# A fused attention-and-MLP kernel: batch 0's q chain reordered with its fifth tile behind the MLP, batch 1 begun on half its tokens, attention placed between halves of second-layer tiles

## The chip, the cores and the metric

The kernel runs on one core of one Trainium2 chip. The metric is the device time of one execution in microseconds (us). Every number quoted as a kernel's time is a median of several executions. Profiled spans are a little shorter than the timed executions of the same kernel (311.2 us of span against 313.3 us of time), and are compared with spans only.

Engines are named as in the profile: PE is TensorE (matmul), PEld its weight load, DVE is VectorE, ACT is ScalarE, POOL is GpSimd, SP is SyncE, whose queue ("SPq") issues most transfers.

## The reference

Linear attention with cosine weights, followed by an MLP with the activation `h * cos(h)`. There are 8 batches, 8 heads, 576 tokens and 64 channels per head.

```python
def _attn_ref(q, k, v):                      # (8, 8, 576, 64) each
    theta = np.pi / 2.0 * pos / S
    def phi(x, c, s):
        r = np.maximum(x, 0.0)
        return np.concatenate([r * c, r * s], axis=-1)      # the "features", 128 wide
    q_p, k_p = phi(q, cos_w, sin_w), phi(k, cos_w, sin_w)
    kv  = np.einsum('bhsf,bhsd->bhfd', k_p, v)
    z   = np.sum(k_p, axis=2)
    num = np.einsum('bhsf,bhfd->bhsd', q_p, kv)
    den = np.einsum('bhsf,bhf->bhs', q_p, z)[..., None] + 1e-06
    return num / den

x = attn_out.transpose(0, 2, 1, 3).reshape(4608, 512)
h = x @ w_in                                  # 512 x 2048, the first layer
g = h * np.cos(h)
out = g @ w_out                               # 2048 x 512, the second layer
```

## The kernel before

A batch of 576 tokens is worked on as four tiles of 128 tokens and a fifth tile of 64. Two batches share the fifth tile: batch `b` uses the even or the odd partitions of tile slot `NT` (`NT` is 4), by `b % 2`. The raw q, k and v of a batch lie in one landing buffer each, which every batch reuses. Here is how it is loaded and read:

```python
raw = {nm: cpool.tile([P, H, NT + 1, D], F32, name=f"{nm}m") for nm in srcs}  # qm, km, vm

def load(b, name, after=None):
    if b >= B:
        return
    m, n = raw[name], b % 2
    if after is not None:          # a tiny copy on POOL that makes the load wait for `after`
        nc.gpsimd.tensor_copy(out=m[0:2, 0, 0, 0:1], in_=after)
    five, four = tokens(srcs[name][b])
    nc.sync.dma_start(out=blocks(m, n), in_=five)                      # 64 partitions, 5 slots
    nc.sync.dma_start(out=blocks(m, 1 - n)[:, :, 0:NT, :], in_=four)   # the others, 4 slots

def feat(b, name, t, g, act):      # relu(x) * cos or sin; reads all 128 partitions of slot t
    dst = (kps if name == "k" else qps)[b][:, t, :, g, :]
    src, sc = raw[name][:, :, t, :], CS[:, b % 2, g, t:t + 1]
    # ... on ScalarE if act, else on VectorE
```

The table `CS` holds zeros for the partitions of slot `NT` that do not belong to the batch, so what they contain makes no difference to the result.

The chain from features to the first layer's input: `q_trans` transposes a q tile on PE and ScalarE evicts it; `num` multiplies it with `kvz` (a `kv_group` evicted by ScalarE), and VectorE divides; `x_trans` transposes x on PE and ScalarE evicts it into `xT`. From batch 2 on (`b >= NPE`, which is 2), both transpositions are done by transfers instead (`q_trans_dma`, `dma_start_transpose`).

```python
def gate(dst, M1):                 # h * cos(h): cosine on ScalarE, product on VectorE
    n = M1.shape[-1]
    ch = apool.tile([P, SM], F32, name="ch", tag="ch", bufs=4)
    nc.scalar.activation(out=ch[:, 0:n], in_=M1, func=AF.Sin, bias=PIH, scale=1.0)
    flush()
    late.append(lambda: nc.vector.tensor_tensor(out=dst, in0=M1, in1=ch[:, 0:n], op=ALU.mult))
```

`moe1` computes one first-layer tile (128 of the 2048 columns for 512 tokens) and calls `gate`; `moe2_main` one second-layer tile.

Batch 0's front:

```python
for hb in range(2):
    kv_group(0, hb)
for t in T1:                       # T1 is the five tiles, T the first four
    feat(0, "q", t, 0, False)
    feat(0, "q", t, 1, t % 2 == 0)
    if t == 1:
        q_trans(0, 0)
q_trans(0, 1)
# ... num and flush in turn with q_trans(0, 2), q_trans(0, 3), x_trans(0, 0)
x_trans(0, 1)
q_trans(0, NT)
weights_in = w_out_sb[0:2, (G - 3) * NJT // G, 0:1]
for name in ("k", "q", "v"):
    load(1, name, weights_in)      # batch 1, once most weights have arrived
for j in range(2):
    moe1(0, j, 0, SM // 2)         # half tiles on the first 256 tokens
x_trans(0, 2)
# ... more half tiles, x_trans(0, 3), then whole tiles
```

The MLP of batch `s` is interleaved with the attention of batch `s + 1` by a list of side work with start times, in us of PE work:

```python
for s in range(1, B + 1):          # b = s + 1
    # main: first-layer tiles of s, with second-layer tiles of s - 1 between them
    side += [(5.5, lambda: q_trans_dma(b)), (5.6, lambda: load(b + 1, "q")),
             (6.4, lambda: load(b + 1, "v")), (11.6, lambda: load(b + 1, "k")),
             (14.0, lambda: kv_group(b, 0)), (14.8, lambda: kv_group(b, 1))]
    side += [(15.7 + 1.2 * t, lambda t=t: num(b, t)) for t in range(NT + b % 2)]
```

PE, DVE, ACT and SP keep the written order. Semaphore waits are put in automatically, by which operations touch the same part of a buffer.

## Time and profile before

| before | |
|---|---|
| time, median of the first 3 runs | 313.34 us (312.91 to 314.59) |
| span of the profiled run | 311.2 us |
| PE busy | 285.3 us, 92% |
| first MLP tile of batch 0 / 1 / 2 / 3 | 23.9 / 60.6 / 92.3 / 125.4 us |
| PE's largest waits after the start | 3.2 us (batch 2's MLP), 1.4 us (batch 1's) |

First the page: busy time of each engine, with its share of the span and its number of instructions, then PE's row and the clock row of the 40 slices (tenths; 7.8 us per slice).

```profile
span 311.2 us, 5548 instructions
PE 285.3 (92%) x2124; PEld 153.9 (49%) x2124; DVE 185.1 (59%) x457; ACT 179.2 (58%) x301; POOL 27.6 (9%) x55
PE   0389999799959999999999999999999999999994
PEclk9999999999998999999999999999999999999999
```

PE is the bottleneck. After the front, its row dips only at slices 8 and 12; the clock dips once, right after the second. (The clock row reads 9 from the start only because the trace records changes of the clock, and nothing before the first. In before, the first is the rise to full at 23.74 us.) The list of PE's waits says what those dips wait for. Columns: waiting instruction, what released it, then total us, count, and the longest.

```profile
PE KV_0_125 L121 <- DVE V_0_71 L114: 11.1, 1, 11.1
PE M_1262 L207 <- DMA xT_819<-x_3_1232: 3.2, 1, 3.2
PE M_823 L207 <- ACT xT_515 L184: 1.4, 1, 1.4
```

The first is the wait for the first k and v. The second is batch 2's MLP waiting for its transposed x. To see why x is late, follow the transfer queue: the timeline of SP before batch 2's start (start us, duration of the issue, queue, line, what).

```profile
69.90 6.19 SPq L129 DMA_TRANSPOSE qT_818<-qp_816  x1
...
79.60 1.79 SPq L96 DMA_DIRECT2D km<-in_k_dram  x1
...
82.89 1.64 SPq L169 DMA_TRANSPOSE xT_819<-x_0_1153  x1
```

The view of transfers gives 7.8 us from issue to landing for that first x tile, which is issued behind the k load, and 2.4 us for the same transposition in the last batch, when the queue is empty:

```profile
xT_819<-x_0_1153 SPq DMA_TRANSPOSE x1, 7.8
...
xT_2954<-x_0_3177 SPq DMA_TRANSPOSE x1, 2.4
```

The Trainium skill ("DMA: Bandwidth & Descriptors", section "Queues, rings and completion order") says that on each engine that moves data, descriptors are consumed in ring order. The two landings above agree with it.

### The profile page before, as it was taken

What the parts mean: (1) busy time and instruction counts of PE and PEld (TensorE: products, weight loads), DVE (VectorE), ACT (ScalarE), POOL (GpSimd) and SP (SyncE); (2) the same over time, 40 slices, a digit from 0 to 9 for tenths busy, and PEclk for the clock granted to TensorE, in tenths of its full rate; (3) what the DMA queues carried; (4) which work ended last, traced back from release to release, by engine and by line L of the source; (5) the groups of instructions that cost most, each with busy time, mean ns of one, the idle gap of its engine ahead of it and who ended that gap; (6) DMA issues with size and microseconds to landing.
All of it is one profiled execution on the core that took longest, in us unless ns stands there. A gap on an engine that the chain in (4) does not pass through costs nothing.

```text
span 311.2 us, 5548 instructions
## 1 busy us (share of the span) xinstructions
PE 285.3 (92%) x2124; PEld 153.9 (49%) x2124; DVE 185.1 (59%) x457; ACT 179.2 (58%) x301; POOL 27.6 (9%) x55
## 2 busy tenths in 40 slices
PE   0389999799959999999999999999999999999994
PEld 0377447445724454445744554446644554447441
DVE  2677790699737665766937565966757581565000
ACT  2679787399407852875557732884458543566111
POOL 0810001100010101010011101010001101010110
PEclk9999999999998999999999999999999999999999
DMA  7999989409990999279934999099937541010121
GB/s 227 305 208 206 326 275 351 155 2 171 334 256 0 140 332 253 90 145 309 275 101 83 239 368 192 1 206 316 211 97 139 135 86 68 1 67 2 67 103 67
DMA packets 78587, 53.76 MB, mean 173 GB/s; under 512 B 47456, under 2 KB 76128, under 8 KB 78560
## 3 DMA queue, kind: packets, MB, share of 16 engines
q1 hardware_dynamic: 71264, 40.51, 54.8%
q0 software_dynamic: 6848, 12.59, 15.5%
q8 instruction: 17, 0.28, 0.4%
q10 hardware_dynamic: 448, 0.31, 0.3%
q14 instruction: 10, 0.08, 0.1%
HBM read 36.74 MB, written 9.44 MB: 148 GB/s over the span
## 4 chain that ended last, share of the span: by engine, by line
PE 79%; ACT 7%; DVE 6%; DMA 5%; issue 2%; SPq 0%; ACTq 0%; DVEq 0%
DMA vm<-in_v_dram 2%; DMA xT_1258<-x_3_1575 1%; ACT ch L197 1%; ACT qT_108 L139 1%; PE M_3707 L233 1%; PE M_3064 L233 1%; PE M_2210 L233 1%; PE M_1726 L233 1%; PE M_2584 L233 1%; PE M_699 L233 1%; PE M_3645 L233 1%; PE M_3489 L233 1%; PE M_2931 L233 1%; PE M_2486 L233 1%; PE M_2140 L233 1%
## 5 line engine op out<-in xcount | busy, mean ns | idle before, releaser
L207 PEld LDWEIGHTS <-w_in_sb 128*128 128x128 f16 x536 | 51.2, 98 | 60.8 <-issue 8.2
L265 POOL DMA_DIRECT2D out_dram<-ost x14 | 7.4, 530 | 211.8 <-ACT ost L259 211.8
L219 PEld LDWEIGHTS <-w_in_sb 128*128 128x128 f16 x256 | 14.7, 98 | 0.9
L121 PE MATMUL KV_0_125<-V_0_71,kp_105 128*128 128x65 f16 x20 | 1.6, 240 | 11.6 <-DVE V_0_71 L114 11.1
L257 DVE COPY ost<-M_3707 128x256 f32<-128x256 f32 x1 | 0.4, 424 | 19.7 <-ACT ost L255 19.7
L112 ACT ACTIVATE V_0_71<-vm 128x512 f16<-128x512 f32 x17 | 10.7, 635 | 0.1
L233 PEld LDWEIGHTS <-g_3357 128*128 128x128 f16 x64 | 6.3, 98 | 7.5
L233 PEld LDWEIGHTS <-g_2957 128*128 128x128 f16 x64 | 6.2, 98 | 7.3
L233 PEld LDWEIGHTS <-g_1654 128*128 128x128 f16 x64 | 6.2, 98 | 7.3
L233 PEld LDWEIGHTS <-g_2512 128*128 128x128 f16 x64 | 6.2, 98 | 7.3
L233 PEld LDWEIGHTS <-g_1261 128*128 128x128 f16 x64 | 6.2, 98 | 7.1
L233 PEld LDWEIGHTS <-g_2099 128*128 128x128 f16 x64 | 6.2, 98 | 7.1
L233 PEld LDWEIGHTS <-g_322 128*128 128x128 f16 x64 | 6.1, 98 | 6.8
L233 PEld LDWEIGHTS <-g_822 128*128 128x128 f16 x64 | 6.0, 98 | 6.9
L112 ACT ACTIVATE V_1_72<-vm 128x512 f16<-128x512 f32 x15 | 9.2, 627 | 0.0
L121 PEld LDWEIGHTS <-kp_105 128*128 128x128 f16 x40 | 2.3, 130 | 11.7 <-ACT kp_105 L104 11.1
L266 POOL DMA_DIRECT2D out_dram<-ost x14 | 7.6, 543 | 0.3 <-issue 0.3
L274 POOL DMA_DIRECT2D out_dram<-ostr x8 | 4.3, 545 | 37.0 <-ACT ostr L271 37.0
L104 ACT ACTIVATE kp_105<-km,CS 128x512 f16<-128x512 f32 x5 | 3.2, 709 | 4.6 <-DMA km<-in_k_dram 4.6
L106 DVE TENSOR_SCALAR kp_105<-km,CS 128x512 f16<-128x512 f32 x5 | 2.1, 483 | 4.7 <-DMA km<-in_k_dram 4.7
L136 PEld LDWEIGHTS <-qp_106 128*128 128x128 f16 x40 | 4.1, 146 | 1.4 <-ACT qp_106 L104 1.2
L207 PE MATMUL M_1262<-xT_819,w_in_sb 128*128 128x512 f16 x4 | 1.9, 620 | 3.2 <-DMA xT_819<-x_3_1232 3.2
(924 smaller groups left out, 752.0 us busy)
## 6 DMA issues: line engine op xcount, KB each, us to landing
out_dram<-ost POOLq DMA_DIRECT2D x28, 256.0 KB, 2.8
km<-in_k_dram SPq DMA_DIRECT2D x8, 640.0 KB, 9.1
vm<-in_v_dram SPq DMA_DIRECT2D x8, 640.0 KB, 8.3
qm<-in_q_dram SPq DMA_DIRECT2D x8, 640.0 KB, 6.7
km<-in_k_dram SPq DMA_DIRECT2D x8, 512.0 KB, 9.6
vm<-in_v_dram SPq DMA_DIRECT2D x8, 512.0 KB, 9.1
qm<-in_q_dram SPq DMA_DIRECT2D x8, 512.0 KB, 7.9
w_in_sb<-in_moe_w_in_dram POOLq DMA_DIRECT2D x4, 512.0 KB, 8.9
```

Of the source, the lines that this page charges most:

```text
L104: nc.scalar.activation(out=dst, in_=src, func=AF.Relu, scale=sc)
L112: nc.scalar.activation(out=dst, in_=src, func=AF.Copy)
L121: nc.tensor.matmul(KV[:, hh, :], lhsT=kps[b][:, t, h].rearrange("p g d -> p (g d)"), rhs=V1[b % 2][:, t, h, :], start=(t == 0), stop=(t == ...
L136: nc.tensor.matmul(QP[:, h, :], lhsT=qps[b][:, t, h].rearrange("p g d -> p (g d)"), rhs=IDENT, is_transpose=True)
L139: nc.scalar.activation(out=qTs[b][:, t], in_=QP, func=AF.Copy)
L197: nc.scalar.activation(out=ch[:, 0:n], in_=M1, func=AF.Sin, bias=PIH, scale=1.0)
L207: nc.tensor.matmul(M1, lhsT=w_in_sb[:, c, j * P:(j + 1) * P], rhs=xts[b][:, c, s0:s1], start=(c == 0), stop=(c == NCT - 1))
L219: nc.tensor.matmul(M1[:, jj, :], lhsT=w_in_sb[:, c, j * P:(j + 1) * P], rhs=xts[("r", pr)][:, c, :], start=(c == 0), stop=(c == NCT - 1))
L233: nc.tensor.matmul(M2, lhsT=gts[key][:, j, gsl], rhs=w_out_sb[:, j, :], start=(j == 0), stop=(j == NJT - 1))
L265: eng.dma_start(out=five[:, t - 1:t + 1, :], in_=blocks(ost, n))
L266: eng.dma_start(out=four[:, t - 1:t + 1, :], in_=blocks(ost, 1 - n))
L274: nc.gpsimd.dma_start(out=five[:, NT, :], in_=blocks(ost, n))
```

## The change

The intent: shorten ScalarE's chain in front of batch 0's MLP by taking the fifth q tile out of it; begin batch 1's MLP after two of its four x tiles; let batch 2's last two x tiles be transposed by PE rather than by the queue; and cut second-layer tiles in halves so that attention work fits more finely between them.

```diff
-            if b >= NPE:
+            if x_by_dma(b, t):              # b > NPE or b == NPE and t < 2
                 nc.sync.dma_start_transpose(out=x_dst(b, t), in_=x16s[(b, t)])
@@ moe2
-            if j == 1:
+            if j == j0 + 1:
                 flush()
@@ batch 0
-        for hb in range(2):
-            kv_group(0, hb)
-        for t in T1:
-            feat(0, "q", t, 0, False)
-            feat(0, "q", t, 1, t % 2 == 0)
-            if t == 1:
-                q_trans(0, 0)
+        kv_group(0, 0)
+        feat(0, "q", 0, 0, False)
+        feat(0, "q", 0, 1, True)
+        kv_group(0, 1)
+        q_trans(0, 0)
+        for t in range(1, NT):
+            for g in range(2):
+                feat(0, "q", t, g, False)
         q_trans(0, 1)
+        q_trans(0, 2)
 # ... q_trans(0, 3) one place earlier too
         x_trans(0, 1)
-        q_trans(0, NT)
         weights_in = w_out_sb[0:2, (G - 3) * NJT // G, 0:1]
-        for name in ("k", "q", "v"):
-            load(1, name, weights_in)
+        load(1, "k", weights_in)
+        load(1, "q", weights_in)
+        load(1, "v", weights_in)
 # ... half tiles of batch 0, unchanged
+        feat(0, "q", NT, 0, False)
+        feat(0, "q", NT, 1, False)
         for j in range(6):
             moe1(0, j, SM // 2, SM)
-        for j in range(6, NJT):
+        for j in range(6, 10):
+            moe1(0, j)
+        q_trans(0, NT)
+        for j in range(10, NJT):
             moe1(0, j)
@@ batch 1
-        for t in T:
-            x_trans(1, t)
+        x_trans(1, 0)
+        x_trans(1, 1)
+        for j in range(2):
+            moe1(1, j, 0, SM // 2)
+        x_trans(1, 2)
+        for j in range(2, 4):
+            moe1(1, j, 0, SM // 2)
+        x_trans(1, 3)
@@ stages s = 1 .. (also, not shown: x_trans(1, NT) at 4.0 instead of 3.0)
+            if s == 1:                       # the other halves of batch 1's first four tiles
+                m1[:4] = [(M1_US / 2, lambda j=j: moe1(1, j, SM // 2, SM)) for j in range(4)]
+            def tile2(b, t):                 # a second-layer tile as two pieces
+                return [(M2_US / 2, lambda u=u: moe2_main(
+                    b, t, u * NJT // 2, (u + 1) * NJT // 2)) for u in range(2)]
 # ... used wherever moe2_main(s - 1, t) and moe2_main(s, t) stood
-                         (14.0, lambda: kv_group(b, 0)), (14.8, lambda: kv_group(b, 1))]
-                side += [(15.7 + 1.2 * t, lambda t=t: num(b, t))
+                         (13.6, lambda: kv_group(b, 0)), (15.0, lambda: kv_group(b, 1))]
+                side += [(16.2 + 1.3 * t, lambda t=t: num(b, t))
                          for t in range(NT + b % 2)]
+                side += [(18.5 + 1.2 * t, lambda t=t: x_trans(b, t))
+                         for t in T if not x_by_dma(b, t)]
```

More of the change, by code (lines that the diff above doesn't have):

```diff
@@ L167, in ratio, with x_by_dma @@
             x16s[(b, t)] = x16.rearrange("p h d -> p (h d)")
-            if b >= NPE:
+            if x_by_dma(b, t):
                 nc.sync.dma_start_transpose(out=x_dst(b, t), in_=x16s[(b, t)])
         late.append(ratio)
+    def x_by_dma(b, t):
+        return b > NPE or b == NPE and t < 2
     def x_dst(b, t):
@@ L323 @@
             val(0, t, t > 2)
-        for hb in range(2):
-            kv_group(0, hb)
-        for t in T1:
-            feat(0, "q", t, 0, False)
-            feat(0, "q", t, 1, t % 2 == 0)
-            if t == 1:
-                q_trans(0, 0)
+        kv_group(0, 0)
[6 more added lines that the diff above has]
+                feat(0, "q", t, g, False)
         q_trans(0, 1)
+        q_trans(0, 2)
         num(0, 0)
         flush()
-        q_trans(0, 2)
+        q_trans(0, 3)
         num(0, 1)
         flush()
-        q_trans(0, 3)
         num(0, 2)
@@ L399 @@
             ahead = 2 if s == 1 else 1
-            m2 = [(M2_US, lambda t=t: moe2_main(s - 1, t))
-                  for t in range(2 if s == 2 else 1, NT)] if s > 1 else []
+            def tile2(b, t):
+                return [(M2_US / 2, lambda u=u: moe2_main(
+                    b, t, u * NJT // 2, (u + 1) * NJT // 2)) for u in range(2)]
+            m2 = [tile2(s - 1, t) for t in range(2 if s == 2 else 1, NT)] if s > 1 else []
             if s > 0 and s % 2 == 0:
-                m2.insert(0, (M2_US, lambda: moe2_rem(s // 2 - 1)))
+                m2.insert(0, [(M2_US, lambda: moe2_rem(s // 2 - 1))])
             main = []
@@ L408 @@
                 if m2 and (n + 1) % per == 0:
-                    main.append(m2.pop(0))
-            main += m2
+                    main += m2.pop(0)
+            main += [f for fs in m2 for f in fs]
             if s < B:
-                main += [(M2_US, lambda t=t: moe2_main(s, t)) for t in range(ahead)]
+                main += [f for t in range(ahead) for f in tile2(s, t)]
             side = []
             if s == 1:
-                side += [(1.0, lambda: num(1, NT)), (3.0, lambda: x_trans(1, NT))]
+                side += [(1.0, lambda: num(1, NT)), (4.0, lambda: x_trans(1, NT))]
             if b < B:
```

## The prediction

> **What bounds it now.** TensorE: the page's busy row gives PE 285.3 of 311.2 us, and the timeline shows it almost gapless from 92 us on (first-layer tile 0.86 us, second-layer tile 3.45). That work is unchanged; only gaps can be won. By the list of waits and the timeline: 11.1 us until the first k and v (untouched); a ragged 12.9 us until the first MLP tile at 23.93; 1.4 us before batch 1's MLP (at 60.63); 0.7 us for the remainder's transpose; 3.16 us before batch 2's MLP (at 92.25), then two tiles in 3.43 us instead of 1.73 at a granted clock of 0.5 (windows); 0.54 us before batch 3's; 0.2 to 0.3 us at each KV group of batches 3 to 7 (1.3 us); 4.4 us of tail (untouched).
>
> **Batch 0.** The MLP waits for ScalarE's serial chain of qT evictions (1.02 us each) and features. The first transpose can start at 14.6 instead of 15.33, q tiles 2 and 4 no longer cost ScalarE 1.3 us mid-chain, and the fifth transpose (0.84) leaves the front; it costs 0.45 later. Estimate: first MLP tile at 21.7; net -2.0 us.
>
> **Batch 1.** In before's time base the first half tile starts after two xT evictions, at 59.65 instead of 60.63; but the second halves need the fourth eviction, now queued behind four half cosines, until about 62.9: 1 us of new gap, a loss of about 0.7, partly repaid as the remainder's transpose no longer waits. Net about 0.
>
> **Batch 2's MLP start** decides the rest. x tiles 2 and 3 move to PE (0.45 us, and two evictions of 0.6). But x tiles 0 and 1 stay on the transfer queue behind the k, q, v loads: tile 0, issued at 82.9, lands only at 90.7, after the loads' traffic ends at 88.5 (DMA windows); tile 1 lands 21.4 us after the q transpose's issue at 69.84. That issue waits for VectorE's last q feature, which now follows eight half gates and three full ones instead of five full: estimate +2.0 us, less the 2.2 won. So tile 1 lands at about 91.1, PE is done at about 87.4: a gap of 3.7 us, no shorter than today, and the clock probably drops again (chance 0.65). The Trainium skill ("TensorE: Matmul & The Clock Gate", Part 1) says an idle window of about 3.4 us halves the clock; this trace agrees (3.16 us of gap, 3.4 us at 0.5). Net -1.1 us cold, -2.7 warm.
>
> **Later batches.** With half tiles, k features reach ScalarE before the eviction that waits for a whole second-layer tile, so KV waits should vanish: -1.0 us. But batch 3's first KV group now precedes its second-layer tile, 1.4 us before its last k feature: up to +1.4, half hidden in the x wait.
>
> **Sum.** -1.4 us (cold) to -3.5 (warm): 310.9 us, range 307.6 to 313.2. Faster by over 2% 0.08, within 2% 0.90, slower 0.02.
>
> **What would show it.** First MLP tile near 21.7; two gaps of about 1 us before batch 1's full tiles; batch 2's q transpose issued near 69.7; PE waiting for x tile 1's DMA, not ScalarE's xT, until 90.5 to 91.5; a KV wait over 1 us at batch 3, none after.
>
> **What would make it wrong.** x tiles 0 and 1 not queued behind the loads, or VectorE done with q earlier: batch 2 starts near 89, warm, and the gain is 5 to 6 us. Conversely a cold clock under the earlier first MLP tiles, or weights not landed, eats up to 1.5 us.

## More of the kernel before

All PE results share 8 PSUM buffers, and the cosines 4 buffers.

Last, what PE and VectorE do around 28 us, where batch 0's MLP has begun (timeline of DVE): the gate products follow their cosines closely. This is the place where the kernel after will look different.

```profile
27.88 0.42 DVE L199 TENSOR_TENSOR g_322<-M_366,ch 128x256 f16<-128x256 f32 x1 [0.43 <-ACT ch L197]
28.25 0.42 DVE L199 TENSOR_TENSOR g_322<-M_374,ch 128x256 f16<-128x256 f32 x1
```

## The result and the profile after

| | before | after |
|---|---|---|
| median (fast runs, 4 each) | 313.95 us (312.91 to 314.59) | 329.06 us (327.84 to 330.61) |
| span of the profiled run | 311.2 us | 326.0 us |
| PE busy | 285.3 us | 284.9 us |
| mean granted clock | 0.993 | 0.971 |

The ratio is 1.0487, with a 95% interval of 1.0429 to 1.0546: slower. All ratios here are the mean time of one kernel's runs over the mean of the other's in the same rounds, so they are not quite the ratios of the medians quoted beside them. Executions over 1.5% slower than the fastest of the same kernel are left out of the means.

The page of the kernel after (the same lines as of before; a slice is now 8.2 us):

```profile
span 326.0 us, 5599 instructions
PE 284.9 (87%) x2148; PEld 154.6 (47%) x2148; DVE 186.3 (57%) x463; ACT 179.6 (55%) x305; POOL 27.7 (8%) x55
PE   0584099988995998999999999999999999999994
PEclk9998579999999799999999999999999999999999
```

PE's work is unchanged. What is new is a slice with no PE work at all, the fifth (33 to 41 us), with the clock at about half. PE's and VectorE's waits (same columns as before) name it:

```profile
PE M_428 L210 <- DVE g_310 L202: 13.3, 1, 13.3
PE KV_0_125 L121 <- DVE V_0_71 L114: 11.7, 2, 11.3
PE M_1304 L210 <- DMA xT_851<-x_1_1236: 4.5, 1, 4.5
PE KV_0_1450 L121 <- ACT kp_1296 L104: 1.3, 1, 1.3
PE M_804 L210 <- ACT xT_515 L187: 1.2, 1, 1.2
PE M_854 L210 <- ACT xT_515 L187: 0.9, 1, 0.9
...
DVE qp_106 L106 <- DMA qm<-in_q_dram: 16.8, 2, 14.9
```

PE waits for a gate product of VectorE, and VectorE waits for a q load. The timeline of the kernel after shows the chain (all engines; the bracket is the idle time before the instruction and what ended it):

```profile
24.78 0.42 DVE L202 TENSOR_TENSOR g_310<-M_354,ch 128x256 f16<-128x256 f32 x1 [0.43 <-ACT ch L200]
...
27.05 1.03 PE L210 MATMUL M_420<-xT_109,w_in_sb 128*128 128x512 f16 x4
...
30.20 0.17 POOL L93 CAST qm<-w_out_sb 2x1 f32<-2x1 f16 x1
...
31.66 0.60 SPq L95 DMA_DIRECT2D qm<-in_q_dram  x1
...
40.13 0.88 DVE L106 TENSOR_SCALAR qp_106<-qm,CS 128x512 f16<-128x512 f32 x2 [14.92 <-DMA qm<-in_q_dram]
40.93 0.42 DVE L202 TENSOR_TENSOR g_310<-M_362,ch 128x256 f16<-128x256 f32 x1
...
41.40 1.01 PE L210 MATMUL M_428<-xT_109,w_in_sb 128*128 128x512 f16 x2 [13.32 <-DVE g_310 L202]
...
41.44 0.47 ACT L200 ACTIVATE ch<-M_396,PIH 128x256 f32<-128x256 f32 x1 [15.02 <-DVE g_310 L202]
```

Read it from the bottom. The two operations at 40.13 are batch 0's fifth-tile features (`qp_106` is batch 0's q features). They wait for a transfer into `qm`, and the only one under way is batch 1's load: gated by the copy on POOL at 30.20 (that is, by the arrival of second-layer weights), issued at 31.66. Behind the features in VectorE's order stand the gate products. Without them no PSUM buffer comes free: from 23.76 us to the stop, PE fills M_362, M_372, M_380, M_388, M_396, M_404, M_412 and M_420, which are all 8 buffers, and it restarts 0.47 us after the product of M_362 began. ScalarE stops too, after the cosines of the first four, which are its 4 buffers.

The clock then costs a little more. It is at half from 30.9 to 44.56 us, and the two tiles after the restart take 3.27 us instead of 1.73.

In the accounts: batch 1's first x transposition moves from 57.83 to 70.20 us, which is +12.37. The stop (13.32) and the cold clock (1.54), less the gain of the shorter front (2.79 us at the first MLP tile, of which 0.3 is given back by the fifth transposition), make the same sum: 13.32 + 1.54 - 2.79 + 0.3 is 12.37. The 0.3 is what this sum leaves over; it was not measured by itself. Batch 1 adds 1.80 us (the lag is 14.17 us at batch 2's MLP), and all the later batches 0.70 (14.87 us at the end).

The start of batch 2's MLP, for comparison with before: the q transposition on SP, the wait on PE, from the two timelines.

```profile
84.19 6.11 SPq L129 DMA_TRANSPOSE qT_850<-qp_848  x1
...
100.05 1.48 SPq L169 DMA_TRANSPOSE xT_851<-x_1_1236  x1
```

```profile
106.42 1.87 PE L210 MATMUL M_1304<-xT_851,w_in_sb 128*128 128x512 f16 x4 [4.46 <-DMA xT_851<-x_1_1236]
```

PE still waits there for the queue, as predicted. The 13.3 us were not predicted at all.

### The profile page after: what moved, and what is told of

Same layout as the page of the kernel before. It is cut to its first block, busy times and chain, and to the rows that moved or that the text cites. A ratio compares the mean times of both kernels' runs of the same rounds, so it can differ in the third digit from the quotient of the medians.

```text
span 326.0 us, 5599 instructions
## 1 busy us (share of the span) xinstructions
PE 284.9 (87%) x2148; PEld 154.6 (47%) x2148; DVE 186.3 (57%) x463; ACT 179.6 (55%) x305; POOL 27.7 (8%) x55
## 4 chain that ended last, share of the span: by engine, by line
PE 66%; DMA 11%; DVE 7%; issue 6%; ACT 4%; POOL 1%; SPq 0%; POOLq 0%; ACTq 0%
DMA qT_1692<-qp_1690 3%; DMA qT_2550<-qp_2548 3%; DMA qm<-in_q_dram 3%; DVE g_803 L202 2%; DMA xT_851<-x_1_1236 2%; ACT ch L200 2%; PE M_2528 L236 1%; PE M_3749 L236 1%; PE M_3040 L236 1%; PE M_2182 L236 1%; PE M_699 L236 1%; PE M_3708 L236 1%; PE M_3531 L236 1%; PE M_2115 L236 1%; PE M_1612 L236 1%
## 5 line engine op out<-in xcount | busy, mean ns | idle before, releaser
L210 PEld LDWEIGHTS <-w_in_sb 128*128 128x128 f16 x552 | 53.2, 99 | 75.0 <-issue 25.8
L222 PEld LDWEIGHTS <-w_in_sb 128*128 128x128 f16 x256 | 14.5, 98 | 0.5
L106 DVE TENSOR_SCALAR qp_106<-qm,CS 128x512 f16<-128x512 f32 x9 | 4.1, 520 | 16.8 <-DMA qm<-in_q_dram 16.8
L210 PE MATMUL M_428<-xT_109,w_in_sb 128*128 128x512 f16 x4 | 1.9, 619 | 13.3 <-DVE g_310 L202 13.3
L236 PEld LDWEIGHTS <-g_3399 128*128 128x128 f16 x64 | 6.2, 98 | 7.6
L236 PEld LDWEIGHTS <-g_2999 128*128 128x128 f16 x64 | 6.2, 98 | 7.3
L236 PEld LDWEIGHTS <-g_1696 128*128 128x128 f16 x64 | 6.2, 98 | 7.3
L236 PEld LDWEIGHTS <-g_2554 128*128 128x128 f16 x64 | 6.2, 98 | 7.3
L236 PEld LDWEIGHTS <-g_2141 128*128 128x128 f16 x64 | 6.1, 98 | 7.1 <-DVE g_2141 L202 0.4
L236 PEld LDWEIGHTS <-g_1303 128*128 128x128 f16 x64 | 6.1, 98 | 6.8
L236 PEld LDWEIGHTS <-g_310 128*128 128x128 f16 x64 | 6.1, 98 | 6.8
L236 PEld LDWEIGHTS <-g_803 128*128 128x128 f16 x64 | 5.7, 98 | 5.7
L121 PEld LDWEIGHTS <-kp_105 128*128 128x128 f16 x40 | 2.3, 130 | 12.0 <-ACT kp_105 L104 11.3
```

The source lines that it names most:

```text
L106: nc.vector.tensor_scalar(out=dst, in0=src, scalar1=0.0, scalar2=sc, op0=ALU.max, op1=ALU.mult)
L121: nc.tensor.matmul(KV[:, hh, :], lhsT=kps[b][:, t, h].rearrange("p g d -> p (g d)"), rhs=V1[b % 2][:, t, h, :], start=(t == 0), stop=(t == ...
L210: nc.tensor.matmul(M1, lhsT=w_in_sb[:, c, j * P:(j + 1) * P], rhs=xts[b][:, c, s0:s1], start=(c == 0), stop=(c == NCT - 1))
L222: nc.tensor.matmul(M1[:, jj, :], lhsT=w_in_sb[:, c, j * P:(j + 1) * P], rhs=xts[("r", pr)][:, c, :], start=(c == 0), stop=(c == NCT - 1))
L236: nc.tensor.matmul(M2, lhsT=gts[key][:, j, gsl], rhs=w_out_sb[:, j, :], start=(j == 0), stop=(j == NJT - 1))
```

## The experiments

The first theory, A, says: the loss is a dependency made by the order in which the kernel is *written*. `feat(0, "q", NT, ...)` is now written below `load(1, "q")`, and reads all 128 partitions of slot `NT`. The load writes 64 of them, so the feature must wait for it, although these 64 are the ones that are multiplied by zero, and the 64 that batch 0 needs are not written in this slot. The rivals say that the new order itself costs the time: features between the gate products, batch 1's half tiles, the moved attention work, or the cold clock.

The built programs could be compared before any run. These are VectorE's instructions 36 to 39 in the kernel after, with their waits (an ordinary listing of the program, not a trace):

```
36 L202 TensorTensor g_310<-M_354,ch 128x256 [waits Activation_49]
37 L106 TensorScalarPtr qp_106<-qm,CS 128x8x64 [waits DMAHW2_49]
38 L106 TensorScalarPtr qp_106<-qm,CS 128x8x64
39 L202 TensorTensor g_310<-M_362,ch 128x256 [waits Activation_49]
```

With the three loads written below the two features, VectorE's order is the same, and the wait on a transfer is gone:

```
36 L202 TensorTensor g_301<-M_345,ch 128x256 [waits Activation_49]
37 L106 TensorScalarPtr qp_106<-qm,CS 128x8x64 x2
38 L202 TensorTensor g_301<-M_353,ch 128x256 [waits Activation_49]
```

The wait is for one of the load's two transfers only, the first (L95), which writes all five slots of its 64 partitions; for the second (L96), which leaves slot `NT` out, the feature does not wait.

Ten kernels were run in three groups, each group on one chip together with before: 313.36 us (e1 to e4), 313.32 us (e5 to e8) and 313.17 us (e9, e10), medians of 11 runs each. All ten gave correct results. The kernels e5, e6 and e7 were profiled more than once; their numbers below are from the profile that is kept (spans 309.7, 309.4 and 306.9 us), where nothing else is said.

| run | median us | ratio to before (95%) |
|---|---|---|
| e1_loads_behind | 313.98 | 1.0035 (0.9996 to 1.0074) |
| e2_only_fifth_late | 326.36 | 1.0434 (1.0377 to 1.0491) |
| e3_q_load_early | 316.59 | 1.0092 (1.0048 to 1.0136) |
| e4_x_by_pe | 310.08 | 0.9899 (0.9856 to 0.9942) |
| e5_whole_m2 | 312.19 | 0.9952 (0.9920 to 0.9983) |
| e6_front_only | 311.71 | 0.9943 (0.9909 to 0.9976) |
| e7_batch1_whole | 309.58 | 0.9875 (0.9838 to 0.9911) |
| e8_together | 307.34 | 0.9809 (0.9779 to 0.9838) |
| e9_halves_old_places | 313.09 | 1.0024 (0.9983 to 1.0065) |
| e10_fifth_in_front | 314.99 | 1.0057 (1.0032 to 1.0083) |

### e1_loads_behind: the kernel after, loads written below the features

```diff
         x_trans(0, 1)
-        weights_in = w_out_sb[0:2, (G - 3) * NJT // G, 0:1]
-        load(1, "k", weights_in)             # and "q", "v"
 # ...
         feat(0, "q", NT, 0, False)
         feat(0, "q", NT, 1, False)
+        weights_in = w_out_sb[0:2, (G - 3) * NJT // G, 0:1]
+        load(1, "k", weights_in)             # and "q", "v"
```

> The changed kernel with its three loads of batch 1 written below the fifth q tile's features instead of above them; the order of the instructions on every engine and queue stays the same. Theory A (the fifth q tile's features, coming after batch 1's q load in the program and reading rows that the load writes, wait for it, VectorE's products stall behind them, PSUM fills and PE stops): PE's 13.3 us wait and the 13.7 us of half clock at 31 us vanish, the span falls by about 14.9 us, to some 313 us (311 to 315), level with before within 1%. Rival B (PE overtook the weights' transfer, or the earlier MLP starves for another reason): the stop remains, 327 to 331 us. Rival C (half tiles and attention inside second-layer tiles cost the time): at most a few us less than 329.

Measured: 313.98 us, back from 329.06, with the same instructions in the same order on every engine. (The two programs differ in a few waits alone: this one, the q load's, which now waits for the features, one later wait of VectorE and three of PE.) The timeline of DVE in e1 shows the features running in their place without a wait:

```profile
24.66 0.42 DVE L202 TENSOR_TENSOR g<-M,ch 128x256 f16<-128x256 f32 x1 [0.43 <-ACT ch L200]
25.00 0.88 DVE L106 TENSOR_SCALAR qp<-qm,CS 128x512 f16<-128x512 f32 x2
25.79 2.40 DVE L202 TENSOR_TENSOR g<-M,ch 128x256 f16<-128x256 f32 x7
```

The clock no longer drops in batch 0. Theory A holds: the wait alone, not the order, made the loss. But e1 is also not faster than before, and PE's waits in e1 name what is left:

```profile
PE M L210 <- DMA xT<-x: 3.5, 1, 3.5
PE M L210 <- ACT xT L187: 2.8, 3, 1.2
PE NUM L150 <- DMA qT<-qp: 2.0, 2, 1.4
PE KV L121 <- ACT kp L104: 1.6, 2, 1.3
```

The start of each batch's MLP (timelines, us) shows where the lead of e1 over before goes:

| MLP of batch | 0 | 2 | 3 | 4 | 5 | 6 | 7 | end |
|---|---|---|---|---|---|---|---|---|
| before | 23.9 | 92.3 | 125.4 | 159.2 | 193.5 | 227.3 | 261.6 | 311.2 |
| e1 | 21.0 | 90.3 | 123.8 | 158.0 | 193.1 | 228.1 | 262.6 | 312.2 |
| lead of e1 | 2.9 | 1.9 | 1.5 | 1.1 | 0.3 | -0.8 | -1.0 | -1.0 |

The front's gain is there, and is given back bit by bit. The runs e4 to e9 ask by what.

### e2_only_fifth_late: before, with nothing but the fifth q tile behind the loads

```diff
-        for t in T1:
+        for t in T:
             feat(0, "q", t, 0, False)
             feat(0, "q", t, 1, t % 2 == 0)
 # ...
-        q_trans(0, NT)
 # ... loads of batch 1, half tiles
+        feat(0, "q", NT, 0, False)
+        feat(0, "q", NT, 1, False)
 # ... q_trans(0, NT) after tile 9
```

> The kernel before with one part of the change alone: the fifth q tile's features and transpose put behind the loads and into the MLP, as the change has them. Theory A: VectorE waits for the q load of batch 1 until about 40 us, PE stands still for 9 to 12 us (it starts its MLP 2 us later than in the changed kernel) and the clock halves: 325 to 329 us. Rivals B and C: within 2 us of before, 312 to 315 us.

Measured: 326.36 us, 1.0434 of before. This one part of the change is enough for nearly all of the loss. Its lines are those of the kernel after (DVE's timeline, then PE's waits):

```profile
40.45 0.88 DVE L106 TENSOR_SCALAR qp<-qm,CS 128x512 f16<-128x512 f32 x2 [13.38 <-DMA qm<-in_q_dram]
```

```profile
PE M L207 <- DVE g L199: 11.8, 1, 11.8
```

The release is at the same time as in the kernel after (40.45 against 40.13 us), because it is the load that sets it; the stop is shorter by 1.5 us, in a run whose first MLP tile is at 22.99 us instead of 21.14.

### e3_q_load_early: the kernel after, its q load first and without the gate

```diff
         weights_in = w_out_sb[0:2, (G - 3) * NJT // G, 0:1]
+        load(1, "q")
         load(1, "k", weights_in)
-        load(1, "q", weights_in)
         load(1, "v", weights_in)
```

> The changed kernel, order of program kept, but batch 1's q load is issued first and without waiting for the second-layer weights, so that it can be issued near 17 us instead of 31.7. Theory A: VectorE's wait ends when this load lands, which I estimate at 24 to 29 us instead of 40, so PE's stop shrinks to 0 to 4 us, and the time to 312 to 318 us. Theory of another cause: 327 us or more.

The dependency stays in this kernel; only the time of what it waits for changes. Measured: 316.59 us. SP's and DVE's timelines:

```profile
17.41 0.60 SPq L95 DMA_DIRECT2D qm<-in_q_dram  x1
```

```profile
27.56 0.88 DVE L106 TENSOR_SCALAR qp<-qm,CS 128x512 f16<-128x512 f32 x2 [2.21 <-DMA qm<-in_q_dram]
```

With the load issued 14.2 us earlier, VectorE's wait falls from 14.92 to 2.21 us, and PE's stop from 13.32 to 0.60. The wait follows the load, as A says. The earlier load has a price: the k and v loads are issued from 34.5 us on instead of 30.1 (in e1), and batch 1's first x transposition comes at 58.2 us instead of 55.0.

### e4_x_by_pe: e1, with all four x tiles of batch 2 transposed by PE

```diff
     def x_by_dma(b, t):
-        return b > NPE or b == NPE and t < 2
+        return b > NPE
```

> As e1, and all four x tiles of batch 2 transposed on PE, none by transfer. My theory of the second loss is that x tiles 0 and 1 sit in the transfer queue behind batch 3's loads (in the changed kernel x tile 1 lands 22.2 us after the q transpose's issue) while PE waits 4.5 us: then the gap before batch 2's MLP shrinks to about 1.5 us, the clock stays full, and batch 2 starts 3 to 5 us earlier than in e1; up to 2 us of it may be lost again before batch 3's MLP, whose x tiles still come by transfer. 1.5 to 5 us less than e1. If the wait was ScalarE's or VectorE's, the time equals e1's.

Measured: 310.08 us, 3.9 us below e1. Batch 2's MLP starts at 88.83 us instead of 90.34, after a wait of 1.22 us for ScalarE instead of 3.53 for the queue. The timeline of PE in e4:

```profile
88.83 3.40 PE L210 MATMUL M<-xT,w_in_sb 128*128 128x512 f16 x15 [1.22 <-ACT xT L187]
```

The clock stays full, and batch 3's start (120.62 us) is 3.2 us ahead of e1's. So two tiles left on the queue were enough to keep the wait that the change wanted to remove.

### e5_whole_m2: e1, with whole second-layer tiles and the old places of KV and num from batch 2's stage on

```diff
             def tile2(b, t):
+                if s > 1:
+                    return [(M2_US, lambda: moe2_main(b, t))]
 # ... for s > 1: KV at 14.0 and 14.8, num at 15.7 + 1.2 * t, as in before
```

> As e1 (313.98 us), but from batch 2's MLP on the second-layer tiles are whole again and the KV and num groups of batches 3 to 7 stand where they stood before the change. In e1 the four stages from batch 3's MLP start to batch 7's took 138.75 us against 136.26 before, and batch 3's KV group waited 1.28 us. If the halves and the moved side work cause that (theory), e5 is 2 to 3.5 us faster than e1, about 311; if my prediction was right that halves save about 1 us there, e5 is some 1 us slower than e1, about 315.

Measured: 312.19 us, 1.8 us below e1, a little less than the 2 to 3.5 us expected. From batch 3's MLP to batch 7's it takes 136.38 us (e1: 138.75; before: 136.26), and the KV wait is back to before's size (PE's waits: total, count, longest):

```profile
PE KV L121 <- ACT kp L104: 1.3, 5, 0.3
```

By these two profiles the halves and the new places together lose 2.4 us over these stages. That is the upper end: in the other profiles the same stretch takes 136.2 to 137.5 us where tiles and places are the old ones (before, e2, e5, e6, e8; mean 136.7), and 136.7 to 138.8 us with the halves and the new places (after, e1, e3, e4, e7, e10; mean 137.7). So the loss is some 1 us on average, in single executions of which two can differ by more. An earlier profile of e5 shows that scatter too: its first MLP tile is at 22.18 us, in the kept one at 20.98 (e1: 21.01), and nothing in the front differs; e7 gave 22.08 and 21.00. The spans of single profiles are therefore not read here to better than 1 us.

### e6_front_only: before, with batch 0's part alone, loads below the features

```diff
 # batch 0 as in the change, then
         feat(0, "q", NT, 0, False)
         feat(0, "q", NT, 1, False)
+        weights_in = w_out_sb[0:2, (G - 3) * NJT // G, 0:1]
+        load(1, "k", weights_in)             # and "q", "v"
```

> The kernel before with batch 0's part of the change alone (q chain reordered, fifth q tile behind the MLP) and the loads below its features. First MLP tile near 21 us instead of 23.9. If batch 2's MLP start hangs on the chain q features, q transpose, loads, x tiles and that chain moves with the rest, the whole gain of about 2.5 us is kept: 310 to 312 us. If the chain is fixed in time by something else (loads of batch 2, second-layer weights), the gain is lost there: 312.5 to 314.

Measured: 311.71 us, ratio 0.9943. The first MLP tile is at 20.87 us and batch 2's MLP at 89.22 (before: 23.93 and 92.25), so the front's 3.1 us are carried through batch 1 whole. (An earlier profile had 21.31 and 89.51, which says the same.) Compare e1, where 1.0 of 2.9 us was lost by then.

### e7_batch1_whole: e1, with batch 1 begun on whole tiles

```diff
-        x_trans(1, 0)
-        x_trans(1, 1)
-        for j in range(2):
-            moe1(1, j, 0, SM // 2)
 # ... and the other halves
+        for t in T:
+            x_trans(1, t)
```

> As e1, but batch 1's MLP begins on whole tiles again (the side work of this stage then falls a little differently among the tiles). Theory of the prediction: the half tiles put VectorE's last q feature about 2 us later, and with it the q transpose, the loads and x tile 1 of batch 2. Then the q transpose is issued 1.5 to 2.5 us earlier than e1's 69.0, and batch 2's MLP starts 1 to 2.5 us earlier than e1's 90.3; time 1 to 2.5 us under e1, if the later stages keep it. If halves cost nothing there, the issue stays at 69.

Measured: 309.58 us, 4.4 us below e1, where 1 to 2.5 us were expected (the two ran on different chips, with before at 313.32 and 313.36 us). SP's timeline and PE's waits:

```profile
67.10 6.19 SPq L129 DMA_TRANSPOSE qT<-qp  x1
```

```profile
PE M L210 <- DMA xT<-x: 2.1, 1, 2.1
```

Batch 2's q transposition is issued 12.07 us after batch 1's first x transposition, against 13.99 in e1 and in the kernel after, and 12.07 in before, too. The half tiles delay VectorE's q features (the last begin at 68.09 us in e1, at 66.16 here), the features delay the q transposition, and everything behind it on the queue is late. With whole tiles the wait at batch 2 falls to 2.1 us, and the clock stays full. Half tiles at batch 1 were a loss. Why it is more than expected was not tested: batch 2's MLP starts 1.7 us earlier than in e1, batch 3's 3.4 us earlier, as the clock stays full, and the rest arises in later stages, whose program is that of e1.

### e8_together: the parts that gained, in one kernel

```diff
 # e1, with the edits of e4, e5 and e7
```

> The loads below the fifth features, batch 1 on whole tiles, all four x tiles of batch 2 by PE, and whole second-layer tiles with the old places of KV and num groups from batch 2's MLP on. From e4 (310.08 us) minus 2 to 3 us for the later stages and minus 1 us for the gap before batch 2's MLP, part of it lost before batch 3's MLP, whose x tiles come by transfer: 305.5 to 308.5 us, faster than before by 2% (1.5 to 2.5). If the parts do not add up, it stays at 309 to 311.

Measured: 307.34 us (306.73 to 308.46), ratio 0.9809 with an interval of 0.9779 to 0.9838: the fastest of all, ahead of before by 1.9%, with 2% inside the interval (305.5 to 308.5 us was expected). Batch 2's MLP begins at 86.87 us without a wait. The timeline of PE in e8, with no bracket at the first-layer matmul:

```profile
84.70 0.61 PE L184 MATMUL XP<-IDENT,x 128*128 128x128 f16 x8
85.15 1.89 PE L236 MATMUL M<-w_out_sb,g 128*128 128x512 f16 x8
86.87 3.40 PE L210 MATMUL M<-xT,w_in_sb 128*128 128x512 f16 x15
```

### e9_halves_old_places: e1, halves kept, KV and num at their old places from batch 3's attention on

```diff
-                         (13.6, lambda: kv_group(b, 0)), (15.0, lambda: kv_group(b, 1))]
-                side += [(16.2 + 1.3 * t, lambda t=t: num(b, t))
+                         (14.0 if s > 1 else 13.6, ...), (14.8 if s > 1 else 15.0, ...)]
+                side += [(15.7 + 1.2 * t if s > 1 else 16.2 + 1.3 * t, lambda t=t: num(b, t))
```

> As e1, second-layer tiles still in halves, but KV and num groups of batches 3 to 7 aimed at the times they had before the change. It parts the two things that e5 took back together (e1 313.98 us, e5 312.19; KV wait of batch 3 1.28 us and q transpose waits of 1.97 us in e1, both gone in e5). If the moved KV and num groups cost the 1.8 us, e9 equals e5, 311.5 to 312.7, and both waits are gone. If the halves themselves cost it, e9 equals e1, 313.4 to 314.6.

Measured: 313.09 us. Against e1 (ratios to before 1.0024 and 1.0035, overlapping intervals) this is inconclusive by time. The trace says more: batch 2's stage is 32.04 us instead of 33.48 and its KV wait is gone, but num now waits for q transpositions four times:

```profile
PE NUM L150 <- DMA qT<-qp: 1.8, 4, 0.6
```

So the moved KV group costs about 1.4 us once (its wait of 1.3 us stands in all six profiles with the new places and in none of the others), and the halves bring num forward to where its q has not landed. How the loss that e5 takes back divides between the two is not settled to better than about 1 us.

### e10_fifth_in_front: e1, the fifth tile's features in the front, only its transposition late

```diff
-        for t in range(1, NT):
+        for t in range(1, NT + 1):
             for g in range(2):
                 feat(0, "q", t, g, False)
 # ... and no features behind the half tiles
```

> As e1, but the fifth q tile's two features stay in front with the others on VectorE; only its transpose is behind the MLP. It asks whether moving the features was needed at all. Worked out from e1's trace: the two features take 0.88 us of VectorE at 17 us, ahead of the first ratios, which decide when the second xT is ready; so the first MLP tile comes 0.5 to 0.9 us later than e1's 21.0 and the time is 0 to 1 us over e1, 314 to 315. If VectorE has room there, it equals e1.

Measured: 314.99 us, first MLP tile at 21.46 us against 21.01 in e1. Moving the features, the very step that made the dependency, bought at most about 0.5 us in the front, which single profiles do not resolve (e4, with the features moved, has 21.38), and the ratios of e1 and e10 overlap. In this profile the clock was at half for 6.8 us around batch 2's start, in e1 for 3.4; that fits the 1.0 us of difference in the medians, but was not tested further.

## Why the prediction was wrong

The prediction said 310.9 us (307.6 to 313.2); the kernel took 329.06.

**The step that failed** stands under "Batch 0": "the fifth transpose (0.84) leaves the front; it costs 0.45 later". It counts the moved tile as work that costs its own time in another place. What the runs showed is a new wait of 14.92 us on VectorE and 13.32 us on PE, for the features of that tile wait for the next batch's load into the same buffer. Moving these alone makes it (e2), taking the dependency away with every order unchanged removes it (e1), and moving the load in time moves it (e3). The list under "What would make it wrong" has no such case: it knew queues, cold clocks and late engines, but not a dependency that did not exist before. It was visible without a run, in the listing of VectorE's waits shown above. The Trainium skill ("Perfetto Trace Analysis", section "Identifying Dependency Chains") advises looking at the semaphores on which an instruction waits; on this program that would have given the wait, though not its length.

**The front otherwise was right.** Predicted: first MLP tile at 21.7, net gain 2.0. Measured: 21.14, and 2.49 net by the account above; in e1, where nothing stops, batch 1's first x transposition comes 2.78 us earlier than in before (55.05 against 57.83). The prediction's reason, ScalarE's shorter chain, is not shown to be all of it: in before PE ran this whole front at half clock, until 23.74 us, while in after the clock rose at 17.25 us. The prediction did not count that, and no run parts the two.

**Batch 1 was right in size.** Two gaps of about 1 us were predicted; they measure 1.2 and 0.9 us.

**Batch 2's start was right.** Predicted: q transposition issued 2.0 us later relative to its stage, and a gap of 3.7 us behind x tile 1 on the queue, start between 90.5 and 91.5 if nothing else went wrong, clock cold. Measured: 1.92 us later; the gap 4.46 us after and 3.53 in e1; start 90.34 in e1, just below the predicted stretch; half clock for 3.4 us in e1. The release was the queue's, not ScalarE's.

**Batch 3's KV wait was right**, over 1 us predicted, 1.3 measured.

**"Later batches: -1.0 us" was wrong too.** From batch 3's MLP to batch 7's, before took 136.26 us, the kernel after 136.74 and e1 138.75. KV waits of about 0.3 us did not vanish everywhere, and new waits for the q transpositions came in (0.5 and 0.35 us after; 0.6 and 1.4 us in e1), since num was brought forward: in before it starts 20.6 us after the MLP of batches 3 and 5 begins, in after 19.1 and 19.0 us after, just as its q lands. e5 takes these back. Over all kept profiles these stages are about 1 us longer with the halves and new places, not 1 us shorter (see e5).

With the dependency mended (e1), the prediction's sum of 310.9 would still have been about 3 us too low; this last term accounts for 2 us of it on average, and for 3.5 us in e1's own profile. Of the 14.87 us between the two spans, the stop and the cold tiles are 14.86; the 2.5 us won in the front are lost again in batch 1 (1.80) and after it (0.70).

**The clock.** The Trainium skill ("TensorE: Matmul & The Clock Gate", Part 1) says that an idle window of about 3.4 us halves the clock. The traces agree on the length: the half-clock stretches measured 3.41 us (before), 13.65 (after), 10.24 (e2) and 6.83 (e3), which are 1, 4, 3 and 2 times 3.41. They do not show that the window has to be wholly idle: before's gap was only 3.16 us, and in e10 the clock fell 2.0 us into the gap, with PE busy for 1.42 of the 3.41 us before. The clock was a follower of the loss here, 1.54 us of it, not its cause.

## What to carry to other kernels

Before an operation is moved down a program, look at every buffer it reads and ask whether the next round's load into it is written above the new place. If so, and if the load writes any part that the operation reads, the operation waits for it, even where that part is multiplied by zero. The same engine order without the wait is had by moving the load's line below it. Compare the waits, not only the order, of the built programs. And where a stage waits on a transfer queue, taking some of the transfers off it gains little while the ones that land last stay behind the same loads.

## What the Trainium skill lacked or had wrong

- "TensorE: Matmul & The Clock Gate", section "Why this matters for your kernels", asks for no gaps over about 3 us, and Part 1 of the same page speaks of an idle window of about 3.4 us. Here a gap of 3.06 us (e6, before batch 2's MLP; half clock from 88.65 to 92.06 us) halved the clock, while gaps of 1.2 to 2.1 us (e4, e7) did not. That fits the first figure; the second is too strict, for in e10 PE had been busy for 1.42 of the 3.41 us before the clock fell.
- The same page, Part 4, says that transposes on TensorE do not engage the full clock. In e4, of the 3.41 us before the clock rose to full at 18.36 us, PE spent 2.96 us on transposes of q and 0.46 us on the small num matmuls. In before, 2.66 us of work in the 3.41 us up to 20.33 us did not raise it, so the num matmuls alone would hardly have done so in e4. Transposes also ran at the full clock once it was there: one every 56 ns, against 107 ns before the rise. No trace has transposes alone in such a stretch.
- "DMA: Bandwidth & Descriptors" has no number for a transposing transfer behind loads in the same queue: 7.8 us from issue to landing here, against 2.4 us in an empty queue.
- No page tells that a read written below the reload of its buffer waits for that load even if the loaded part is of no use to it (a matter of how the program is built, not of the chip): 13.3 us of PE here.
